# Causal attention then a cosine MLP: every transposition as a pair of 64-row halves, one reciprocal a step, three probability buffers

## The chip, the cores and the metric

The kernel runs on one core of a Trainium2 chip. The metric is the device time of one execution in microseconds (us): median of 3 runs before the change 608.6, lowest 608.53, highest 608.68.

A core has five engines that the text speaks of: PE (TensorE, matrix products and transpositions, which write to the eight banks of the accumulation memory PSUM), DVE (VectorE), ACT (ScalarE), POOL (GpSimd, which here works in SBUF only) and SP, which issues most DMAs. Each takes its instructions in the order written; they meet only through semaphores.

## The reference, cut to what matters

```python
# q, k, v: 4 batches x 12 heads x 448 rows x 64
scores = scale * q @ k.T                      # per batch and head
scores = where(above the diagonal, -1e9, scores)
attn = exp(scores - max(scores)); attn /= attn.sum() + 1e-9
x = (attn @ v)                                # heads side by side: 1792 x 768
h = x @ w_in                                  # 768 x 2048
out = (h * cos(h)) @ w_out                    # 1792 x 768
```

## The kernel before, in words

The work has two stages. The attention stage takes 24 steps, one for each batch and pair of heads; then the MLP stage, a long dense sequence of products on PE, uses the rest of the time. The change touches the attention stage alone. Its order is written out by hand, engine by engine, by the order of the calls in the loop at L477; no scheduler moves anything.

A step treats the 448 rows of two heads in seven row blocks `m` = 1 to 7 of 64 rows each; one head's 64 rows and the other's share the 128 partitions. Block `m` has `64*m` columns, since later keys are masked. The parts of a step `i`, with their names in the code:

- `transpose_in` (L307): PE turns q and k (loaded by `load_qk`, 112 partitions by four rows each) with four transpositions of 112 rows each; `evac_in` (L319) copies each 128x448 result from PSUM to SBUF. In step `i` this is done for step `i+1`.
- `scores` (L345): 16 products q k^T, into banks 4 to 7. Each stands in the trace as two matrix instructions.
- `masked` (L360): DVE adds the mask, writes the block to `prob` and takes the row maxima, one instruction for each block. `exps` (L368): ACT takes the exponential in place and sums the rows.
- `inverse` (L376): DVE adds 1e-9 to the sums and takes the reciprocal, two small instructions; done twice a step, for the blocks `FIRST` = (7, 4, 3) in their own step and for `SECOND` = (6, 1, 5, 2) early in the next. `normalise` (L381): POOL multiplies each block by its reciprocals.
- `tp` (L400): in step `i` PE transposes the 14 squares of 128x128 of step `i-1`'s probabilities, in four groups `ORDER`; `evac_tp` (L408) copies each group out: two of 512 columns on DVE, one of 512 and one of 256 on ACT.
- `av` (L421): in step `i` PE multiplies the transposed probabilities of step `i-2` by v; `finish_hi` (ACT) and `finish_lo` (DVE) split the result.
- At the end of a step the loop yields; the caller (L1357) then puts one half of a weight conversion on DVE (L139 and L142, or L148 and L152), and what is left of it goes to POOL in the next step (`postponed`).

Two `prob` tiles are used in turn. After step 23 the first products of the MLP (`fill`, L464) are put between the remaining parts.

## Time and profile before

| | us |
|---|---|
| median of 3 runs | 608.6 |
| profiled execution, time | 608.03 |
| its span, first to last instruction | 606.2 |
| PE, DVE, ACT, POOL busy in the span | 595.4, 475.7, 409.0, 455.1 |
| granted PE clock, mean | 0.999 of 2.4 GHz |

The attention stage takes about the first 160 us. The profile's views are read thus: a timeline has one row for an instruction, or for a run of equal ones of one engine: start, duration, engine, source line, operation, tiles, shapes, count, and in brackets the idle time before it with what ended it. Instructions of one engine overlap: the next one starts before the last has drained, so what one costs its engine is the distance from its start to the next start. "PEld" are PE's weight loads, which go ahead of the products.

### The profile page before, as it was taken

Reading aid. Unit: us, or ns where it says so; the run is one execution under the profiler, and the core shown is the slowest. Engines: PE = TensorE matmul, PEld = TensorE weight load, DVE = VectorE, ACT = ScalarE, POOL = GpSimd, SP = SyncE. Lnnn points to the kernel's source line nnn. Section 1 sums busy time; section 2 is a strip of 40 time slices with the busy share of each in tenths; the row PEclk is TensorE's granted clock in tenths of the full one; section 3 lists DMA queues with packets and bytes.
Section 4 is the critical chain, followed back from the end, with each engine's and each line's share of the span. In section 5 each row is a group of like instructions: output and inputs, shape, how many; then the busy total and the mean of one; then the engine's idle time right before and its main releaser. Section 6 shows DMA issues by size and latency. Waiting matters only on the chain.

```text
span 606.2 us, 13434 instructions
## 1 busy us (share of the span) xinstructions
PE 595.4 (98%) x4786; PEld 546.6 (90%) x4786; DVE 475.7 (78%) x1020; ACT 409.0 (67%) x925; POOL 455.1 (75%) x527
## 2 busy tenths in 40 slices
PE   7999999999999999999999999999999999999996
PEld 6788888888799998999999999999999999999995
DVE  5999999999477787777777777853387887887786
ACT  4899999999666787777778777632544643654540
POOL 2778887888358788877878777844588778878894
PEclk9999999999999999999999999999999999999999
DMA  6757667758046869796968879589979548658104
GB/s 145 175 132 179 164 141 195 167 137 236 10 138 234 297 228 347 241 340 199 337 241 286 297 225 323 194 323 393 407 297 306 196 148 288 214 168 298 51 0 157
DMA packets 127010, 134.18 MB, mean 221 GB/s; under 512 B 75072, under 2 KB 111280, under 8 KB 126944
## 3 DMA queue, kind: packets, MB, share of 16 engines
q1 hardware_dynamic: 119264, 106.92, 56.4%
q0 software_dynamic: 4928, 24.78, 11.1%
q10 hardware_dynamic: 2752, 1.64, 0.9%
q8 instruction: 38, 0.62, 0.4%
q14 instruction: 28, 0.23, 0.1%
HBM read 83.36 MB, written 49.94 MB: 220 GB/s over the span
## 4 chain that ended last, share of the span: by engine, by line
PE 75%; DVE 21%; issue 2%; DMA 1%; POOL 0%; ACTq 0%; ACT 0%; DVEq 0%; POOLq 0%
PE banks L678 22%; PE banks L1107 13%; PE banks L1127 13%; DVE pb L363 9%; PE banks L583 7%; PE banks L584 7%; PE banks L582 7%; DVE pm L315 4%; PE banks L1144 2%; PE banks L1031 2%; DVE ct L148 1%; DVE xa L460 1%; DVE stat L379 1%; DVE ct L152 1%; DVE ct L139 1%
## 5 line engine op out<-in xcount | busy, mean ns | idle before, releaser
L666 DVE TENSOR_TENSOR acc<-acc,banks 128x768 f32<-128x768 f32 (+1 forms) x122 | 112.7, 932 | 43.3 <-PE banks L678 33.0
L385 POOL TENSOR_TENSOR pb<-pb,stat 128x448 f32<-128x448 f32 (+6 forms) x166 | 101.9, 643 | 34.3 <-DVE stat L379 32.4
L678 PE MATMUL banks<-w,gh 128*128 128x384 f32 x512 | 109.8, 335 | 0.0
L371 ACT ACTIVATE pb<-pb,stat 128x448 f32<-128x448 f32 (+6 forms) x168 | 84.8, 507 | 14.7 <-DVE stat L363 9.4
L678 PEld LDWEIGHTS banks<-w,gh 128*128 128x128 f32 x512 | 90.8, 188 | 1.6 <-DVE acc L666 0.2
L583 PE MATMUL banks<-xa,w 128*128 128x512 f32 x192 | 75.2, 391 | 0.0
L584 PE MATMUL banks<-xa,w 128*128 128x512 f32 x192 | 75.0, 391 | 0.0
L582 PE MATMUL banks<-xa,w 128*128 128x512 f32 x192 | 74.8, 390 | 0.0
L678 PE MATMUL banks<-w,gl 128*128 128x384 f32 x256 | 65.1, 335 | 0.0
L702 POOL TENSOR_TENSOR w<-ct,w 128x768 fp32r<-128x768 f32 x28 | 51.9, 1852 | 14.6 <-ACT w L701 9.4
L363 DVE CUSTOM_DVE_ANT_0 pb<-banks,mask 128x448 f32<-128x448 f32 (+6 forms) x168 | 61.3, 417 | 1.7 <-PE banks L354 1.6
L590 ACT ACTIVATE ni<-banks 128x512 int32<-128x512 f32 (+1 forms) x64 | 34.5, 538 | 32.9 <-PE banks L584 19.1
L609 POOL TENSOR_TENSOR gl<-r,gh 128x512 fp32r<-128x512 f32 x32 | 41.5, 1299 | 19.3 <-ACT gh L608 19.1
L592 DVE SCALAR_TENSOR_TENSOR r<-ni,banks 128x512 f32<-128x512 int32 (+1 forms) x56 | 35.0, 626 | 21.4 <-ACT ni L590 20.7
L403 PE MATMUL banks<-ident,pb 128*128 128x128 f32 x336 | 48.0, 277 | 1.6 <-POOL pb L385 0.9
L594 ACT ACTIVATE r<-r 128x512 f32<-128x512 f32 (+1 forms) x56 | 32.8, 586 | 21.7 <-DVE r L592 21.0
L678 PEld LDWEIGHTS banks<-w,gl 128*128 128x128 f32 x256 | 46.4, 188 | 0.0
L597 DVE SCALAR_TENSOR_TENSOR r<-r,banks 128x512 f32<-128x512 f32 (+1 forms) x56 | 35.1, 626 | 13.9 <-ACT r L595 13.9
L1107 PE MATMUL banks<-xb,bb 128*128 128x384 f32 x234 | 44.7, 334 | 0.0
L354 PE MATMUL banks<-flat 64*64 64x64 f32 (+5 forms) x768 | 42.6, 356 | 1.2 <-DVE stat L379 0.7
L354 PEld LDWEIGHTS banks<-flat 64*64 64x64 f32 x768 | 30.8, 133 | 13.6 <-issue 2.5
L584 PEld LDWEIGHTS banks<-xa,w 128*128 128x128 f32 x192 | 36.0, 188 | 7.5
(139 smaller groups left out, 1492.9 us busy)
## 6 DMA issues: line engine op xcount, KB each, us to landing
bb<-w_in_d SPq DMA_DIRECT2D x48, 384.0 KB, 5.0
land<-in_moe_w_in_dram SPq DMA_DIRECT2D x14, 768.0 KB, 5.5
land<-in_moe_w_out_dram SPq DMA_DIRECT2D x14, 768.0 KB, 5.1
w_out_d<-w POOLq DMA_DIRECT2D x14, 768.0 KB, 5.5
big<-w_out_d SPq DMA_DIRECT2D x25, 384.0 KB, 4.6
w_in_d<-w POOLq DMA_DIRECT2D x7, 768.0 KB, 4.1
raw_d<-ct POOLq DMA_DIRECT2D x14, 384.0 KB, 7.3
land<-in_k_dram SPq DMA_DIRECT2D x46, 112.0 KB, 3.2
```

What stands on the lines that cost most here:

```text
L354: nc.tensor.matmul(place(m)[heads(j ^ SWAP[m]), c : c + z - a], lhsT=qt[heads(j), (m - 1) * R : m * R], rhs=kt[heads(j), a:z], start=banks ...
L363: nc.vector.tensor_tensor_reduce(out=probs(i, m), in0=place(m), in1=mask[:, z : z + m * R], scale=-scale, scalar=3.0e38, op0=ALU.add, op1= ...
L371: nc.scalar.activation(probs(i, m), probs(i, m), AF.Exp, scale=-1.0, bias=st[:, 0, col(m)], accum_out=st[:, 1, col(m)],)
L385: eng.tensor_tensor(p, p, r.to_broadcast(list(p.shape)), op=ALU.mult)
L582: yield nc.tensor.matmul(hv, lhsT=wh[:, f], rhs=x[:, 0, cc, t], start=(cc == 0), stop=False)
L583: yield nc.tensor.matmul(hv, lhsT=wh[:, f], rhs=x[:, 1, cc, t], start=False, stop=False)
L584: yield nc.tensor.matmul(hv, lhsT=wl[:, f], rhs=x[:, 0, cc, t], start=False, stop=(cc == NCC - 1))
L666: nc.vector.tensor_tensor(d, d, o, op=ALU.subtract)
L678: nc.tensor.matmul(o[:, e, 0:EH], lhsT=a[:, cs], rhs=w[:, e * EH : (e + 1) * EH], start=(x == 0), stop=(x == 5),)
L702: nc.gpsimd.tensor_tensor(w[:, 1], tf, f32(w[:, 0]), op=ALU.subtract)
L1107: nc.tensor.matmul(o, lhsT=w[:, u, k * P : (k + 1) * P], rhs=x[k][:, v], start=k + m == 0, stop=k == K - 1 and m == 2,)
L1127: nc.tensor.matmul(o[:, b % 2, 0:EH], lhsT=g_ops[i][u][:, c * P : (c + 1) * P], rhs=wouts[g, i][:, v], start=(x == 0), stop=(x == 2),)
```

## The change

- q and k are loaded on 64 partitions by seven rows each, q on the lower half of the partitions and k on the upper half. `transpose_in` does seven pairs of transpositions of 64 rows; the two of a pair use the two halves of PE's rows and write different banks. It is done two steps ahead (for step `i+2` in step `i`), and the copies out of PSUM, both on ACT, open step `i+1`.
- `tp` is done likewise: each square becomes two transpositions of 64 rows on the two halves, 28 in all, in two groups of seven squares; each group fills two banks, copied out by four copies of 448 columns, two on DVE and two on ACT.
- `inverse` is called once a step, for all seven blocks, when the last `exps` is done; all seven `normalise` follow it. Steps 0 and 1 are written out apart. Three `prob` tiles are used in turn.
- The blocks are taken in the order 4, 3, 7, 6, 5, 1, 2. Up to step 22 the loop yields in the middle of the step, so the weight conversion on DVE stands behind the last `masked`.

```diff
-                nat[i] = [nat_t[0:Q4, 2 * (i % 3) + x] for x in range(2)]
+                nat[i] = nat_t[:, i % 3]
...
-            def transpose_in(i, which, b):
-                for c in range(4):
-                    nc.tensor.transpose(o[:, c], nat[i][which][:, c], ident[0:Q4, 0:Q4])
+            def transpose_in(i, bs, order=None):
+                for c, h in order or [(c, h) for c in range(NM) for h in range(2)]:
+                    o = qkt[i, h][1].rearrange("p (r c) -> p c r", c=NM)
+                    nc.tensor.transpose(o[:, c], nat[i][half(h), c], ident[half(h), half(h)])
...
-            FIRST, SECOND = (7, 4, 3), (6, 1, 5, 2)
+            FIRST, SECOND = (4, 3, 7), (6, 5, 1, 2)
+            ALL = FIRST + SECOND
...
+            GROUPS = [
+                [(6, 0), (7, 0), (6, 1), (7, 1), (6, 2), (7, 2), (3, NM)],
+                [(2, 0), (4, 0), (3, 0), (5, 0), (4, 1), (5, 1), (5, NM)],
+            ]
...
+            def tp(i, g, bs):
+                for x, (m, kc) in enumerate(GROUPS[g]):
+                    for h in range(2):
+                        nc.tensor.transpose(
+                            banks8[:, bs[h], x * R : (x + 1) * R],
+                            prob[i][half(h), a * R : (a + 2) * R], ident[half(h), half(h)],
+                        )
...
+            TB_, G1, G2 = (2, 3), (7, 4), (5, 6)
...
+                elif cur:
+                    if i + 1 < N:
+                        evac_in(i + 1, 0)
+                        evac_in(i + 1, 1)
+                    masked(i, 4, 3, 7, 6, 5, 1, 2)
+                    exps(i, 4, 3, 7, 6, 5)
+                if i < N - 1:
+                    yield i
...
+                if old:
+                    av(i - 2)
+                    finish_hi(i - 2)
+                    finish_lo(i - 2)
+                if cur:
+                    exps(i, 5, 1) if i == 1 else exps(i, 1)
+                if prev:
+                    open_ptr(i - 1)
+                    tp(i - 1, 0, G1)
+                    evac_tp(i - 1, 0, G1, 0, True)
+                    evac_tp(i - 1, 0, G1, 1)
+                if cur:
+                    exps(i, 2)
+                if 1 < i < N - 2:
+                    transpose_in(i + 2, TB_)
+                if prev:
+                    tp(i - 1, 1, G2)
+                    evac_tp(i - 1, 1, G2, 1)
+                if cur:
+                    inverse(i, ALL)
+                    normalise(i, 6, 7, 3, 5, 4, 1, 2)
+                if prev:
+                    evac_tp(i - 1, 1, G2, 0, True)
```

On DVE, before, from the end of one step into the next (`xa`: the attention result, `pm`: transposed probabilities, `ct`: weights, `pb`: `prob`; the row named ISA is `masked`):

```order
L460 TENSOR_TENSOR xa<-banks,xa 128x448
L315 COPY pm<-banks 128x512 x2
L139 TENSOR_SCALAR ct<-st 128x256
L142 SCALAR_TENSOR_TENSOR ct<-st,ct 128x256
L363 ISA pb_145,stat<-banks,mask 128x448
L363 ISA stat 128x1
L378 TENSOR_SCALAR stat<-stat 128x4
L379 RECIPROCAL stat<-stat 128x4
```

The same place after it:

```order
L139 TENSOR_SCALAR ct<-st 128x256
L142 SCALAR_TENSOR_TENSOR ct<-st,ct 128x256
L457 TENSOR_TENSOR xa<-banks,xa 128x448
L317 COPY pm<-banks 128x448
L378 TENSOR_SCALAR stat<-stat 128x7
L379 RECIPROCAL stat<-stat 128x7
L317 COPY pm<-banks 128x448
L363 ISA pb_144,stat<-banks,mask 128x256
```

The conversion has moved ahead of the copies, the two copies are shorter, and the one `inverse` stands between them.

On ACT, one whole step before, from its first exponential to the next step's (`flat`: turned q or k):

```order
L371 ACTIVATE pb_145,stat<-pb_145,stat 128x448
L371 ACTIVATE pb_145,stat<-pb_145,stat 128x256
L371 ACTIVATE pb_145,stat<-pb_145,stat 128x192
L456 CAST xa<-banks 128x448
L317 COPY flat<-banks 128x448
L371 ACTIVATE pb_145,stat<-pb_145,stat 128x384
L317 COPY flat<-banks 128x448
L371 ACTIVATE pb_145,stat<-pb_145,stat 128x64
L371 ACTIVATE pb_145,stat<-pb_145,stat 128x320
L317 COPY pm<-banks 128x512
L371 ACTIVATE pb_145,stat<-pb_145,stat 128x128
L317 COPY pm<-banks 128x256
```

And after:

```order
L371 ACTIVATE pb_146,stat<-pb_146,stat 128x256
L371 ACTIVATE pb_146,stat<-pb_146,stat 128x192
L371 ACTIVATE pb_146,stat<-pb_146,stat 128x448
L371 ACTIVATE pb_146,stat<-pb_146,stat 128x384
L371 ACTIVATE pb_146,stat<-pb_146,stat 128x320
L453 CAST xa<-banks 128x448
L371 ACTIVATE pb_146,stat<-pb_146,stat 128x64
L319 COPY pm<-banks 128x448
L371 ACTIVATE pb_146,stat<-pb_146,stat 128x128
L319 COPY pm<-banks 128x448
L319 COPY flat<-banks 128x448 x2
```

The copies of q and k now stand behind the last exponential, next to the last copy of `pm`.

On PE, a step's transpositions before, between `av` and the next `scores` (`land`: q or k as loaded):

```order
L440 MATMUL banks<-pm,vn_89 64x128 x6
L311 MATMUL banks<-ident,land 128x112 x4
L403 MATMUL banks<-ident,pb_144 128x128 x4
L311 MATMUL banks<-ident,land 128x112 x4
L403 MATMUL banks<-ident,pb_144 128x128 x10
L354 MATMUL banks<-flat 64x64 x2
```

And after:

```order
L437 MATMUL banks<-pm,vn_89 64x128 x6
L402 MATMUL banks<-ident,pb_146 128x64 x14
L313 MATMUL banks<-ident,land 128x64 x14
L402 MATMUL banks<-ident,pb_146 128x64 x14
L354 MATMUL banks<-flat 64x256 x2
```

22 transpositions have become 42 with half the columns.

## Rows read from the trace of the kernel before

**Rows 1.** Busy time of PE, PEld, DVE, ACT, POOL, 40 to 140 us; clock, DMA.

```profile
40.00:140.00 100.00, 99.94 (x1608) 83.52 (x1610) 97.67 (x380) 92.68 (x321) 84.03 (x141) 1.00 0.66 162
```

**Rows 2.** The chain that ended last, share of the span by engine.

```profile
PE 75%; DVE 21%; issue 2%; DMA 1%; POOL 0%; ACTq 0%; ACT 0%; DVEq 0%; POOLq 0%
```

**Rows 3.** Timeline of DVE through one step; start us, us, instruction.

```profile
73.40 0.61 DVE L363 CUSTOM_DVE_ANT_0 pb<-banks,mask 128x448 f32<-128x448 f32 x1
...
73.94 0.16 DVE L378 TENSOR_SCALAR stat<-stat 128x4 f32<-128x4 f32 x1
...
74.25 0.42 DVE L363 CUSTOM_DVE_ANT_0 pb<-banks,mask 128x256 f32<-128x256 f32 x1
...
74.60 0.35 DVE L363 CUSTOM_DVE_ANT_0 pb<-banks,mask 128x192 f32<-128x192 f32 x1
...
76.93 1.28 DVE L315 COPY pm<-banks 128x512 f32<-128x512 f32 x2
78.12 0.76 DVE L148 SCALAR_TENSOR_TENSOR ct<-st,ct 128x256 uint32<-128x256 uint32 x1
...
79.45 0.61 DVE L363 CUSTOM_DVE_ANT_0 pb<-banks,mask 128x448 f32<-128x448 f32 x1
```

**Rows 4.** Timeline of DVE: the first `masked` of steps 2 and 23.

```profile
18.54 0.62 DVE L363 CUSTOM_DVE_ANT_0 pb<-banks,mask 128x448 f32<-128x448 f32 x1
...
146.27 0.61 DVE L363 CUSTOM_DVE_ANT_0 pb<-banks,mask 128x448 f32<-128x448 f32 x1
```

**Rows 5.** DVE's copies out of PSUM: duration ns min/median/max.

```profile
L315 DVE COPY pm<-banks x48: 661/681/692, 17.4 to 157.6; 128x512 f32<-128x512 f32 x48
L315 DVE COPY flat<-banks x4: 608/618/626, 6.5 to 15.9; 128x448 f32<-128x448 f32 x4
```

**Rows 6.** Timeline of ACT through the same step.

```profile
74.05 0.67 ACT L371 ACTIVATE pb<-pb,stat 128x448 f32<-128x448 f32 x1 [0.42 <-DVE stat L363]
...
77.11 0.52 ACT L317 COPY flat<-banks 128x448 f32<-128x448 f32 x1
77.53 0.36 ACT L371 ACTIVATE pb<-pb,stat 128x64 f32<-128x64 f32 x1
...
78.41 0.58 ACT L317 COPY pm<-banks 128x512 f32<-128x512 f32 x1
78.88 0.41 ACT L371 ACTIVATE pb<-pb,stat 128x128 f32<-128x128 f32 x1
79.18 0.20 ACT L371 ACTIVATION_READ_ACCUMULATOR pb<-pb,stat 128x1 f32 x1
```

**Rows 7.** Timeline of PE in the same step: products on halves, transpositions, scores.

```profile
73.56 0.22 PE L429 MATMUL banks<-pm,vn 64*64 64x64 f32 x2
73.56 0.22 PE L429 MATMUL banks<-pm,vo 64*64 64x64 f32 x2
73.62 0.22 PE L429 MATMUL banks<-pm,vn 64*64 64x64 f32 x2
...
75.31 0.60 PE L311 MATMUL banks<-ident,land 112*128 112x112 f32 x4
...
76.70 1.40 PE L403 MATMUL banks<-ident,pb 128*128 128x128 f32 x10
78.03 1.74 PE L354 MATMUL banks<-flat 64*64 64x64 f32 x32
```

**Rows 8.** Timeline of PE's weight loads there: two for transpositions behind a wait.

```profile
77.66 0.20 PEld L403 LDWEIGHTS banks<-ident,pb 128*128 128x128 f32 x2 [0.16 <-DVE pm L315]
```

**Rows 9.** Timeline of POOL in the same step: `normalise`.

```profile
74.45 2.12 POOL L385 TENSOR_TENSOR pb<-pb,stat 128x384 f32<-128x384 f32 x4 [0.62 <-DVE stat L379]
...
77.10 2.15 POOL L385 TENSOR_TENSOR pb<-pb,stat 128x448 f32<-128x448 f32 x3
```

**Rows 10.** Timeline at both ends of the stage: step 1 on DVE; PE's weight loads in step 24.

```profile
13.77 1.08 DVE L385 TENSOR_TENSOR pb<-pb,stat 128x64 f32<-128x64 f32 x2
...
153.72 0.42 PEld L403 LDWEIGHTS banks<-ident,pb 128*128 128x128 f32 x4 [0.35 <-POOL pb L385]
```

More of the change, by code (lines that the diff above doesn't have):

```diff
@@ L236, in attention @@
             NM = S // R
-            Q4 = S // 4
-            nat_t = rows.rearrange("p (t c d) -> p t c d", t=6, d=P)
+            nat_t = rows[:, 0 : 3 * NM * P].rearrange("p (t c d) -> p t c d", t=3, d=P)
             vn_t = [cst.tile([P, NB, P], F32, name=f"vn{i}") for i in range(3)]
@@ L249, in heads, with half @@
                 return slice(j * D, (j + 1) * D)
+            def half(h):
+                return slice(h * R, (h + 1) * R)
             def load_qk(i, *engs):
                 b, hp = pairs[i]
-                nat[i] = [nat_t[0:Q4, 2 * (i % 3) + x] for x in range(2)]
-                for dst, src in zip(nat[i][::-1], (k, q)):
+                nat[i] = nat_t[:, i % 3]
+                for h, src in ((1, k), (0, q)):
                     for j, eng in enumerate(engs or (nc.sync, nc.sync)):
                         eng.dma_start(
-                            out=dst[:, :, heads(j)],
-                            in_=src[b, 2 * hp + j].rearrange("(p c) d -> p c d", c=4),
+                            out=nat[i][half(h), :, heads(j)],
+                            in_=src[b, 2 * hp + j].rearrange("(p c) d -> p c d", c=NM),
                         )
@@ L291, in attention @@
             make_identity(nc, ident)
-            prob_t = [cst.tile([P, NM * (NM + 1) // 2 * R], F32, name=f"pb{i}") for i in range(2)]
+            prob_t = [cst.tile([P, NM * (NM + 1) // 2 * R], F32, name=f"pb{i}") for i in range(3)]
             mask = cst.tile([P, S + W], F32, name="mask")
@@ L317, in evac, with evac_in @@
                     nc.scalar.copy(dst, src)
-            def evac_in(i, which, dve=False, rs=slice(0, Q4)):
-                d, s = qkt[i, which]
-                d = d.rearrange("p (r c) -> p r c", c=4)
-                s = s.rearrange("p (r c) -> p r c" if which else "p (c r) -> p r c", c=4)
-                evac(d[:, rs], s[:, rs], dve)
+            def evac_in(i, h, dve=False):
+                evac(*qkt[i, h], dve)
             AT = {5: 0, 1: 5, 3: 6, 7: 9, 6: 16, 4: 22, 2: 26}
@@ L334, in open_step @@
             def open_step(i):
-                prob[i] = prob_t[i % 2]
+                prob[i] = prob_t[i % 3]
                 stats[i] = at.tile([P, 3, 8], F32, tag="stat", bufs=3, name="stat")
@@ L469, in fill, with tail @@
                     pass
-            transpose_in(0, 1, 7)
+            def tail(i, *ms):
+                inverse(i, ms)
+                normalise(i, *ms)
+            TB_, G1, G2 = (2, 3), (7, 4), (5, 6)
+            transpose_in(0, TB_, [(c, 1) for c in range(NM)])
             evac_in(0, 1)
             keep_warm(14)
-            transpose_in(0, 0, QB)
+            transpose_in(0, TB_, [(c, 0) for c in range(NM)])
             evac_in(0, 0, True)
             keep_warm(8)
+            load_qk(2)
             for i in range(N + 4):
-                cur, prev, nxt = i < N, 0 < i <= N, i + 1 < N
-                old = 0 <= i - 2 < N
-                if i + 2 < N:
-                    load_qk(i + 2)
+                cur, prev, old = i < N, 0 < i <= N, 0 <= i - 2 < N
+                if i >= N - 1:
+                    G1, G2 = (2, 3), (4, 5)
+                if i + 3 < N:
+                    load_qk(i + 3)
                 if prev:
@@ L486, in attention @@
                     scores(i)
[L487 to L488 removed]
                 if i == 0:
                     masked(i, 4, 3)
[L491 to L496 removed]
+                    exps(i, 4, 3)
+                    masked(i, 7, 6)
+                    exps(i, 7)
@@ L574, in attention @@
-                yield i
+                    normalise(i, 7, 3, 4)
+                    exps(i, 5, 1, 2)
+                    transpose_in(2, (0, 1))
+                    yield i
+                    continue
+                if i == 1:
+                    masked(i, 4, 3, 7, 6)
+                    inverse(i - 1, SECOND)
+                    normalise(i - 1, *SECOND)
+                    masked(i, 5, 1, 2)
+                    evac_in(2, 0, True)
+                    evac_in(2, 1, True)
+                    exps(i, 4, 3, 7, 6)
+                elif cur:
[4 more added lines that the diff above has]
+                    exps(i, 4, 3, 7, 6, 5)
@@ L576, in m1_sum @@
+                if i >= N - 1:
+                    yield i
     def m1_sum(ring, g, fi, t0, n, hv):
```

136 lines of the change are left out of this document (28 added, 108 removed).

## The prediction

> **What bounds the kernel now.** I read four views in this order. First the busy times of a steady stretch of the attention stage, 40 to 140 us [rows 1]: PE is shown busy for 99.94 of 100 us, VectorE (DVE) for 97.67, ScalarE (ACT) for 92.68, POOL for 84.03. PE's figure overlaps pipelined products, so it does not settle who binds. Then the chain that ended last [rows 2]: DVE holds 21% of the span, 127 us, though in the dense MLP stage PE carries the chain; so in the attention stage it runs through DVE. Then DVE's timeline [rows 3]: from one first `masked` at 73.40 to the next at 79.45 are 6.05 us with instruction after instruction and no idle time noted. Last, the start of the first `masked` of step 2 and of step 23 [rows 4]: 127.73 us for 21 steps, 6.08 each. The steady stage is bound by DVE's own work, with ACT about 0.45 us a step behind it and PE able to follow.
>
> **The change, part by part.**
>
> *DVE loses 0.43 us a step.* An `inverse` (two instructions) costs from 73.94 to 74.25, 0.30 us beside what any hand-over takes [rows 3]; one of two goes. Its three or four columns become seven, which I cost at nothing: it is the fixed part of a small instruction. The two copies of `pm` take 1.19 us of DVE (76.93 to 78.12), 0.60 each; a copy of 448 columns is 0.06 shorter than one of 512 (618 against 681 ns) [rows 5], so two save 0.13. DVE alone would then need 6.05 - 0.43 = 5.62 us a step. The moved weight conversion costs DVE the same wherever it stands.
>
> *ACT gains 0.1 us a step.* Its copies out of PSUM were two of 448, one of 512 and one of 256; they become four of 448. A 448 takes 0.42 (77.11 to 77.53), a 512 0.47 (78.41 to 78.88) [rows 6]; the 256 is an estimate of 0.3, between half and the whole of a 448; so the sum goes from 1.6 to 1.7 us.
>
> *A ring between DVE and ACT closes.* The single `inverse` waits for the last exponential of its own step, and behind it on DVE wait the last copy of `pm`, the next step's `masked` and so ACT's next exponentials. The ring: `masked` of block 4, 74.25 to 74.60, 0.35; its read-out and the hand-over to ACT, 0.11 (the 448 block leaves DVE at 73.94 and ACT starts at 74.05) [rows 3, 6]; ACT from its first exponential to the end of its last; hand-over to DVE, taken as half of the 0.11; `inverse` 0.30; a 448 copy, 0.60 - 0.06 = 0.53. ACT's part is read from its stretch 74.05 to 79.38 (79.18 + 0.20), 5.33 us, which holds seven exponentials, the cast of the result, two 448 copies and a 512 [rows 6]. In the new order only one 448 copy stands inside, so 5.33 - 0.42 - 0.47 = 4.44. Sum: 0.35 + 0.11 + 4.44 + 0.05 + 0.30 + 0.53 = 5.78 us. That is above DVE's own 5.62, so it sets the step: 0.30 less than 6.08, and over the 21 steps 6.3 us. DVE then waits some 0.16 us a step at `inverse`.
>
> *PE's transpositions: off the path, but their price must be bounded.* Before, 22 of them, each 0.11 us from start to start (four in 0.60 with 0.27 for one), take with their waits from 75.31 to 78.03, 2.72 us of the step; all else of PE takes 6.05 - 2.72 = 3.33 [rows 7]. The nearest rows for pairs on two halves are the 64-row products of L429: the upper-half product (`vo`) starts at the same 73.56 as the lower (`vn`), and the next lower one 0.06 later. So 21 pairs would cost 21 x 0.06 = 1.3 us, and PE would need 4.6 to 5.0 us a step. The other end: halves that take turns, 42 x 0.06 = 2.5 us. I take the first, as the row shows both halves at work at once; being of 64 columns, it does not show it for loads of 128. Since PE isn't in the ring, its 1 us saved counts for nothing.
>
> The Trainium skill says so of such a change in general (TensorEngine Tiling (Array Packing), PSUM Bottleneck): tiling makes TensorE faster, not the copies out of PSUM. Here the trace agrees as far as it goes, DVE at 97.67 of 100; a sum that credited PE's saving would be 21 us lower.
>
> *POOL* has the same seven `normalise`, now in one batch of 2.12 + 2.15 = 4.3 us [rows 9], and the same rest of the weights. Its load is 0.84 x 6.08 = 5.1 us a step [rows 1], under 5.78, and the three `prob` tiles let `tp` of a step wait for it until the middle of the next. I cost it at nothing; if that cover went, POOL's lateness would hold up PE's second group and then ACT's last copy.
>
> *SP and the loads.* Same number of loads, one step more of them at the start, with landings a step ahead of use: nothing.
>
> *The ends of the stage.* Step 1 loses two `normalise` on DVE, 1.08 us [rows 10]; I take 1.1 off. At the end the seven `normalise` of step 23 stand before `tp` of that step, where PE already waited 0.35 us for four of them [rows 10]: POOL has 2 us more to do before the last square, but PE has products of the MLP to put there and DVE reaches that `inverse` earlier. Between a loss of 2 and a gain of 1, nearest to the row: 0.
>
> *Sum* against the profiled execution's own time, 608.0: 608.0 - 6.3 - 1.1 = 600.6. The median of the runs is 0.6 above that execution, so 601.2 us.
>
> **The rivals.**
>
> *A wait through PE closes a longer ring (slower).* DVE's last copy of `pm` frees bank 5; if all the next scores came behind it, the ring would be: copy 0.62, scores and `av` 3.33, then on ACT the cast 0.42, an exponential 0.36, a copy 0.42 and the last exponential 0.50, `inverse` 0.30, and three hand-overs of 0.1: 6.25 us a step, 0.17 x 21 = 3.6 us more, and without the gain in step 1 612.2 us. It decides from the point at which more than half of the scores wait for that copy: by the new order the first five of eight blocks' products go to banks that are freed earlier, and what stands behind is block 6, 2 and 1, some 0.75 of the 1.5 us of scores, which makes the ring 5.5. For it: bank 5 is the last freed, and block 6, which goes there, is the fourth that `masked` asks for. Against: 0.28 us of room. If it binds in part, a step is near 5.95: 605.
>
> *The halves take turns (slower).* PE would need 3.33 + 42 s + 0.39 of waits as now (2.72 - 22 x 0.106): with s = 0.06, 6.24 us a step, so + 3.4 - 1.1: 610.9 us. It decides from s = 0.056 upwards. Against: the pair at 73.56. For: no row has loads of 128 columns on two halves.
>
> The Trainium skill has a rule that would make it far worse (TensorE: Matmul & The Clock Gate, LDWEIGHTS): a weight load takes its columns at 1.2 GHz, whatever its rows, so 0.107 us for 128 columns; 42 in turn would be 4.5 us and the kernel near 650, and if the halves' loads overlap, 2.25 us and the forecast stands. The trace speaks against the figure: two such loads stand within 0.20 us at 0.14 each, so the second began 0.06 after the first [rows 8].
>
> *PE was the bound after all.* Then a step loses the whole 1.0 to 1.4 us: 21 us or more, 586. For it, 99.94 of 100; against it, DVE's row without a gap. *The change of PE's load lowers its clock*: the granted clock is 1.00, of 2.4 GHz, in the stretch [rows 1], and the pauses to come are under 1 us; I give it nothing of its own.
>
> *DVE alone binds*, ACT slipping out of the ring by running ahead: 5.62 us, 597.8; it lies in the forecast's own range.
>
> **How the numbers follow.** Chances: the DVE-ACT ring or a little beside it, 0.78 (own range 597.8 to 604.4: steps of 5.62 to 5.90, where the last has the first 0.7 us of the start lost); the ring through PE, 0.12, of which three quarters in part (605) and the rest in full (612); halves in turn 0.08; PE bound 0.02. The range, 597.8 to 605.8, leaves out the slower cases and PE's. A difference under 0.2%, 1.2 us, can't be told from none: same is 607.4 to 609.8. Faster: 0.77 + 0.07 + 0.02 = 0.86; same 0.06, from parts of both slower cases; slower 0.08.
>
> **What would show it.** Right: steps of 5.7 to 5.9 us from first `masked` to first `masked`; a wait of DVE for ACT before L378 or of ACT for DVE before the first exponential, and little else; lower and upper halves of L402 starting within 0.01 us of each other, pairs 0.06 apart; PE with idle time in each step; the MLP stage's length unchanged. Wrong: `masked` or the cast of the result waiting for PE (the longer ring), transpositions 0.06 apart singly (turns), DVE still without a gap at 6.0 us or more (its instructions grew), or `tp` waiting for POOL in each step.

## The result, and the profile after

| | us |
|---|---|
| predicted | 601.2 (597.8 to 605.8) |
| measured, median of 4 runs | 614.14 (611.85 to 614.63) |
| against before (608.62) | ratio 1.0080, 95% interval 1.0064 to 1.0096 |
| profiled execution, time and span | 614.63 and 612.6 |

The kernel became 0.8% slower. The spans differ by 6.4 us, in three places. The first `masked` of steps 2 and 23 stand in DVE's timeline after the change thus (start, duration, instruction):

```profile
20.11 0.42 DVE L363 CUSTOM_DVE_ANT_0 pb<-banks,mask 128x256 f32<-128x256 f32 x1 [1.12 <-PE banks L354]
...
150.35 0.42 DVE L363 CUSTOM_DVE_ANT_0 pb<-banks,mask 128x256 f32<-128x256 f32 x1 [0.43 <-PE banks L354]
```

Against [rows 4]: the start took 1.57 us more (20.11 against 18.54), the 21 steps 2.51 more (130.24 against 127.73, 6.20 a step instead of 6.08), and from there to the end of the span 2.34 more (462.2 against 459.9).

**The steady steps.** Busy time of the same 100 us as [rows 1], same columns:

```profile
40.00:140.00 100.00, 84.81 (x1924) 72.40 (x1916) 88.75 (x347) 92.63 (x316) 84.84 (x139) 1.00 0.70 165
```

DVE fell from 97.67 to 88.75 and PE from 99.94 to 84.81; ACT stands where it was. No engine is full, and yet a step is longer: it goes round in a ring, a chain of waits over several engines that comes back one step later to the instruction it began with. One step on DVE after the change, where [rows 3] showed no gap:

```profile
73.62 0.62 DVE L457 TENSOR_TENSOR xa<-banks,xa 128x448 fp32r<-128x448 f32 x1 [0.33 <-ACT xa L453]
74.17 0.61 DVE L317 COPY pm<-banks 128x448 f32<-128x448 f32 x1
74.78 0.17 DVE L378 TENSOR_SCALAR stat<-stat 128x7 f32<-128x7 f32 x1
74.98 0.20 DVE L379 RECIPROCAL stat<-stat 128x7 f32<-128x7 f32 x1
75.10 0.57 DVE L317 COPY pm<-banks 128x448 f32<-128x448 f32 x1
76.02 0.42 DVE L363 CUSTOM_DVE_ANT_0 pb<-banks,mask 128x256 f32<-128x256 f32 x1 [0.34 <-PE banks L354]
...
79.78 0.62 DVE L457 TENSOR_TENSOR xa<-banks,xa 128x448 fp32r<-128x448 f32 x1 [0.18 <-ACT xa L453]
```

DVE waits twice: 0.33 for ACT's cast ahead of the subtraction L457, and 0.34 for PE ahead of the first `masked`. PE and ACT in the same step, answering to [rows 6, 7] (PE's first and last row are cut off by the window, at 12 and 8 of 14):

```profile
72.80 0.53 PE L313 MATMUL banks<-ident,land 64*128 64x64 f32 x12
73.61 0.65 PE L402 MATMUL banks<-ident,pb 64*128 64x64 f32 x14 [0.28 <-POOL pb L385]
74.83 1.81 PE L354 MATMUL banks<-flat 64*64 64x256 f32 x29 [0.57 <-DVE pm L317]
...
78.35 0.65 PE L402 MATMUL banks<-ident,pb 64*128 64x64 f32 x14
78.83 0.60 PE L313 MATMUL banks<-ident,land 64*128 64x64 f32 x14
79.92 0.46 PE L402 MATMUL banks<-ident,pb 64*128 64x64 f32 x8 [0.48 <-POOL pb L385]
```

```profile
76.48 0.51 ACT L371 ACTIVATE pb<-pb,stat 128x256 f32<-128x256 f32 x1 [0.46 <-DVE stat L363]
...
79.23 0.52 ACT L453 CAST xa<-banks 128x448 fp32r<-128x448 f32 x1
```

PE is idle 0.57 us until DVE's copy of `pm` frees bank 7. The ring can be read off these rows: subtraction 0.55 (73.62 to 74.17), first copy 0.61, hand-over 0.05, from the first product of the scores to the first `masked` 1.19 (74.83 to 76.02), to ACT 0.46, five exponentials 2.75 (76.48 to 79.23), cast and hand-over 0.55, and the next subtraction starts at 79.78: 6.16 us. Counted from `masked` to `masked`, steps of 6.04 and 6.21 take turns in the first half of the stage; most of the difference is that in every other step `masked` follows the first product after 1.07 instead of 1.19. The same rows confirm what was said of PE: 14 transpositions on two halves take 0.65 and 0.60 us, where ten of the old ones took 1.40.

**The start.** PE in step 1, and the granted clock of three stretches (the last three columns are the clock as a share of 2.4 GHz, the DMA share, GB/s):

```profile
13.59 0.65 PE L313 MATMUL banks<-ident,land 64*128 64x64 f32 x14
16.03 0.86 PE L402 MATMUL banks<-ident,pb 64*128 64x64 f32 x14 [1.80 <-POOL pb L385]
17.32 1.01 PE L402 MATMUL banks<-ident,pb 64*128 64x64 f32 x14 [0.42 <-POOL pb L385]
```

```profile
9.50:16.28 6.78, 4.74 (x104) 3.87 (x95) 6.32 (x35) 6.54 (x25) 3.10 (x5) 1.00 0.74 146
16.28:23.10 6.82, 6.40 (x90) 5.16 (x88) 4.93 (x21) 5.36 (x19) 5.03 (x10) 0.50 0.64 153
23.10:30.00 6.90, 6.53 (x158) 5.70 (x156) 5.47 (x22) 5.85 (x20) 4.31 (x7) 1.00 0.69 159
```

PE stood idle 1.80 us for POOL, and right behind that pause the clock fell to half (1.2 GHz) for 6.8 us. Before, PE stood 0.94 at this place, and the clock is 1.00 in all three stretches; the row and the middle one of the three:

```profile
14.76 0.88 PE L403 MATMUL banks<-ident,pb 128*128 128x128 f32 x6 [0.94 <-POOL pb L385]
```

```profile
16.28:23.10 6.82, 6.75 (x101) 5.31 (x100) 6.70 (x29) 5.92 (x21) 4.71 (x8) 1.00 0.79 187
```

The 1.57 us are not all of one kind. The first `masked` of step 0 already starts at 9.27 instead of 8.33; in the other kernels built on the changed one it does so anywhere between 8.57 and 9.58, by their profiled executions, and the pause comes only later. From the first `masked` of step 1 to that of step 3, a stretch that holds the pause and the half clock, it is 14.02 us after the change, against 12.78 before. Three of the four executions of the new kernel have a mean clock of 0.992 to 0.994 over the span, the fastest, 611.85, has 0.996; before has 0.999.

**The rest** is in the MLP stage, most of it late: counted from step 23, ACT's instructions run about 0.9 us behind those of the kernel before from 260 to 437 us, and 2.6 behind from 450 on. Between 437 and 456 us POOL waits 2.1 us for `raw` to land, DVE 1.3 for `xb`; the second wait stands in e3_warm too, whose stage is 2 us shorter.

```profile
POOL tr L1043 <- DMA raw<-raw_d: 2.1, 1, 2.1
...
DVE acc L646 <- DMA xb<-t_d: 1.3, 1, 1.3
```

### The profile page after: what moved, and what is told of

Its sections match the earlier page's. It is cut to its first block, busy times and chain, and to the rows that moved or that the text cites. A ratio compares the mean times of both kernels' runs of the same rounds, so it can differ in the third digit from the quotient of the medians.

```text
span 612.6 us, 14289 instructions
## 1 busy us (share of the span) xinstructions
PE 580.3 (95%) x5266; PEld 534.8 (87%) x5266; DVE 464.2 (76%) x972; ACT 411.4 (67%) x925; POOL 459.0 (75%) x529
## 3 DMA queue, kind: packets, MB, share of 16 engines
q10 hardware_dynamic: 2752, 1.64, 1.0%
## 4 chain that ended last, share of the span: by engine, by line
PE 70%; ACT 14%; DVE 10%; DMA 2%; POOL 2%; issue 2%; SPq 0%; DVEq 0%; ACTq 0%; POOLq 0%
PE banks L660 17%; PE banks L1109 12%; PE banks L1089 12%; ACT pb L371 10%; PE banks L565 6%; PE banks L566 6%; PE banks L564 6%; PE banks L354 4%; PE banks L1126 2%; PE banks L1013 2%; DVE pm L317 2%; DVE pb L363 2%; DVE xa L457 2%; DMA big<-w_out_d 1%; ACT xa L453 1%
## 5 line engine op out<-in xcount | busy, mean ns | idle before, releaser
L385 POOL TENSOR_TENSOR pb<-pb,stat 128x448 f32<-128x448 f32 (+6 forms) x168 | 104.7, 658 | 34.8 <-DVE stat L379 33.0
L371 ACT ACTIVATE pb<-pb,stat 128x256 f32<-128x256 f32 (+6 forms) x168 | 84.2, 504 | 14.7 <-DVE stat L363 14.7
L363 DVE CUSTOM_DVE_ANT_0 pb<-banks,mask 128x256 f32<-128x256 f32 (+6 forms) x168 | 60.0, 420 | 9.5 <-PE banks L354 9.5
L354 PE MATMUL banks<-flat 64*64 64x64 f32 (+5 forms) x768 | 45.6, 368 | 11.7 <-DVE pm L317 11.2
L354 PEld LDWEIGHTS banks<-flat 64*64 64x64 f32 x768 | 35.7, 136 | 21.6 <-DVE pm L317 13.3
L1109 PE MATMUL banks<-big,gh 128*128 128x384 f32 x168 | 42.6, 334 | 0.0
```

What stands on the lines that cost most here:

```text
L354: nc.tensor.matmul(place(m)[heads(j ^ SWAP[m]), c : c + z - a], lhsT=qt[heads(j), (m - 1) * R : m * R], rhs=kt[heads(j), a:z], start=banks ...
L363: nc.vector.tensor_tensor_reduce(out=probs(i, m), in0=place(m), in1=mask[:, z : z + m * R], scale=-scale, scalar=3.0e38, op0=ALU.add, op1= ...
L371: nc.scalar.activation(probs(i, m), probs(i, m), AF.Exp, scale=-1.0, bias=st[:, 0, col(m)], accum_out=st[:, 1, col(m)],)
L385: eng.tensor_tensor(p, p, r.to_broadcast(list(p.shape)), op=ALU.mult)
L1109: nc.tensor.matmul(o[:, b % 2, 0:EH], lhsT=g_ops[i][u][:, c * P : (c + 1) * P], rhs=wouts[g, i][:, v], start=(x == 0), stop=(x == 2),)
```

## The experiments

Medians; the ratio is to the kernel before in the same batch. Step 2: start of its first `masked`; step: mean of the 21 behind it, both from the profiled execution.

| run | us | ratio, 95% | step 2 | step |
|---|---|---|---|---|
| before | 608.6 | | 18.54 | 6.08 |
| after | 614.14 | 1.0080 (1.0064 to 1.0096) | 20.11 | 6.20 |
| e1_4_3_first | 610.91 | 1.0029 (1.0009 to 1.0050) | 19.83 | 6.15 |
| e2_copy_first | 606.41 | 0.9955 (0.9939 to 0.9972) | 19.85 | 5.89 |
| e12_both | 604.44 | 0.9927 (0.9910 to 0.9945) | 18.92 | 5.90 |
| e3_warm | 610.06 | 1.0020 (1.0010 to 1.0029) | 18.75 | 6.16 |
| e4_copy_first_warm | 604.79 | 0.9925 (0.9909 to 0.9942) | 19.28 | 5.90 |
| e5_turns | 611.40 | 1.0037 (1.0024 to 1.0050) | 19.00 | 6.16 |
| e6_two_inverses | 612.60 | 1.0061 (1.0046 to 1.0076) | 19.25 | 6.26 |
| e7_bank7_by_act | 603.88 | 0.9917 (0.9902 to 0.9931) | 18.28 | 5.89 |
| e8_bank7_no_add | 601.68 | 0.9879 (0.9862 to 0.9897) | 18.23 | 5.87 |
| e9_warm_no_add | 609.38 | 1.0016 (1.0005 to 1.0027) | 18.83 | 6.16 |
| e10_before_no_add | 603.37 | 0.9917 (0.9899 to 0.9935) | 18.07 | 5.87 |
| e11_4_with_2 | 612.60 | 1.0070 (1.0054 to 1.0086) | 20.85 | 6.19 |
| e13_4_2_first | 609.77 | 1.0019 (1.0010 to 1.0029) | 21.73 | 6.03 |
| e14_v_first | 601.51 | 0.9879 (0.9863 to 0.9896) | 18.48 | 5.74 |
| e15_inverse_sooner | 612.10 | 1.0052 (1.0037 to 1.0067) | 18.17 | 6.16 |
| e16_all | 602.97 | 0.9893 (0.9872 to 0.9915) | 18.19 | 5.74 |

### Is it the ring through the first copy?

e2_copy_first moves one call on the changed kernel; e12_both adds the edit of e1.

```diff
                     finish_hi(i - 2)
-                    finish_lo(i - 2)
...
                     evac_tp(i - 1, 0, G1, 0, True)
+                if old:
+                    finish_lo(i - 2)
...
```

> On DVE the first copy of pm goes ahead of the subtraction of the result (L457), nothing else is moved. Theory (ring through the first copy): the subtraction's 0.55 us, its wait of 0.33 for ACT's cast and the cast leave the ring, so the scores of the next step may start up to 0.8 us sooner; a step falls to about 5.8 us, where ACT's own 5.75 holds it: about 606. Rival P (POOL and PE's second group): no change, 614. Rival L (last copy): no change, the last copy keeps its place.

> Both edits: products of blocks 4 and 3 first, and the first copy of pm ahead of the subtraction. Theory: the ring through PE is then far below ACT's own 5.75 us and below the DVE-ACT ring of 5.78 that was forecast, so little beyond either edit alone: steps of about 5.75 to 5.8, 605. Rival P: 614. If a ring of another kind remains in each single edit, this one falls below both.

Steps of 5.89 and 5.90 instead of 6.20, for one DVE instruction put behind its neighbour. In the 6.20 stands one step of 6.89 at half clock; with the clock kept in both (e4_copy_first_warm against e3_warm) it is 5.90 against 6.16, 0.26 less. The rivals of POOL and of the last copy predicted no change. DVE's wait has changed its place; in e12_both it stands where the prediction had put it:

```profile
78.06 0.41 DVE L363 CUSTOM_DVE_ANT_0 pb<-banks,mask 128x256 f32<-128x256 f32 x1
...
81.51 0.61 DVE L317 COPY pm<-banks 128x448 f32<-128x448 f32 x1
82.04 0.61 DVE L457 TENSOR_TENSOR xa<-banks,xa 128x448 fp32r<-128x448 f32 x1
83.02 0.17 DVE L378 TENSOR_SCALAR stat<-stat 128x7 f32<-128x7 f32 x1 [0.36 <-ACT pb L371]
83.22 0.20 DVE L379 RECIPROCAL stat<-stat 128x7 f32<-128x7 f32 x1
83.34 0.57 DVE L317 COPY pm<-banks 128x448 f32<-128x448 f32 x1
83.86 0.42 DVE L363 CUSTOM_DVE_ANT_0 pb<-banks,mask 128x256 f32<-128x256 f32 x1
```

```profile
78.57 0.51 ACT L371 ACTIVATE pb<-pb,stat 128x256 f32<-128x256 f32 x1 [0.16 <-DVE stat L363]
...
82.79 0.19 ACT L371 ACTIVATION_READ_ACCUMULATOR pb<-pb,stat 128x1 f32 x1
```

From `masked` at 78.06 to `masked` at 83.86 it is 5.80 us, through ACT (78.57 to 82.98) and the one `inverse`, for which DVE waits 0.36. Both edits together gave no shorter step than the second alone, as expected if another ring then binds; but the 5.75 to 5.8 expected for it are met only by every other step (5.80 and 5.96 in turn).

e7_bank7_by_act leaves the subtraction where it was and frees bank 7 otherwise (on e3_warm, with e1's order of products):

```diff
-            TB_, G1, G2 = (2, 3), (7, 4), (5, 6)
+            TB_, G1, G2 = (2, 3), (4, 7), (5, 6)
```

> On e3_warm with the products in the order of e1_4_3_first: the two banks of the first group of transpositions are exchanged, so that ACT's copy (some 0.3 us sooner in the trace of the changed kernel) frees bank 7 and DVE's first copy, still behind the subtraction, frees bank 4. Theory (the ring closes because blocks 4 and 3, the first that masked asks for, wait in bank 7 for DVE's first copy, and masked waits for both): steps fall to about 5.9 us with the subtraction where it was, 604.5 us. Rival (e2_copy_first gained because DVE no longer stood 0.33 us before the subtraction waiting for ACT's cast): no change against e3_warm, 610.

5.89 us, 603.88. Two different cuts of the same ring give the same step, and e1's order of products, which e7 has besides, is worth 0.06 by itself (below); that the ring ran through bank 7 and DVE's first copy is shown.

### What lies in the 1.19 us from products to `masked`?

```diff
-                    (4, 0, 0, 4 * R), (7, 0, 6 * R, 7 * R), (7, R, 0, 6 * R), (3, 0, 0, 3 * R),
+                    (4, 0, 0, 4 * R), (3, 0, 0, 3 * R), (7, 0, 6 * R, 7 * R), (7, R, 0, 6 * R),
```

> The products of the scores go in the order 4, 3, 7, 7, 5, 6, 2, 1 instead of 4, 7, 7, 3, ... Theory (the ring of 6.16 us a step goes through the subtraction L457, the FIRST copy of pm, the scores of the blocks in bank 7, the first masked and ACT's exponentials): the first masked no longer waits for the 448 columns of block 7; it starts about 0.77 us after the first product instead of 1.19, so a step falls from 6.20 to about 5.8 us (ACT's own work, 0.926 x 6.20 = 5.75 us, is the next floor), 21 x 0.4 = 8 us: about 606. Rival P (PE's second group of transpositions, which waits for POOL's normalise in every step, sets the step): no change, 614. Rival L (DVE's last copy of pm, bank 5): no change, since block 6 stays where it is in the row of products.

A miss: 0.06 us a step, not 0.4. The first `masked` starts 1.13 us after the first product (87.42 against 86.29). The products that PE started in the first 0.2 us tell why (L354, durations in ns, span of the starts, shapes with counts):

```profile
L354 PE MATMUL banks<-flat x8: 218/347/485, 86.3 to 86.5; 64*64 64x64 f32 x4, 64*64 64x256 f32 x2, 64*64 64x384 f32 x2
```

Both parts of block 7 (64 and 384 columns) have begun, and nothing of block 3 (192 columns), which stands ahead of them in the program. Blocks 4 and 3 use the same two quarters of the array and follow one another; block 7 uses the other two and runs beside them. Read from the single records, block 3's last product ends 0.97 us after the first one of the step, here as in the changed kernel: its place in the program had not delayed it. The next two runs exchange blocks 2 and 3 in PSUM, so that 4 has the shorter neighbour; e13 issues that neighbour ahead of 7. Both have the thirty products of e3_warm (see The start).

```diff
-            BANK = {..., 2: (6, 5), 4: (7, 0), 3: (7, 4)}
+            BANK = {..., 2: (7, 4), 4: (7, 0), 3: (6, 5)}
...
-                    (4, ...), (7, ...), (7, ...), (3, ...), (5, ...), (6, ...), (2, ...), (1, ...),
+e11:                (4, ...), (7, ...), (7, ...), (2, ...), (5, ...), (6, ...), (3, ...), (1, ...),
+e13:                (4, ...), (2, ...), (7, ...), (7, ...), (5, ...), (6, ...), (3, ...), (1, ...),
...
-                    masked(i, 4, 3, 7, 6, 5, 1, 2)
-                    exps(i, 4, 3, 7, 6, 5)
+                    masked(i, 4, 7, 6, 5, 3, 1, 2)
+                    exps(i, 4, 7, 6, 5, 3)
```

> On e3_warm: blocks 2 and 3 exchange their places in PSUM, so block 4 shares its bank with block 2 (128 columns) and no longer with 3 (192); masked and the exponentials take 3 behind 5. Theory (masked of block 4 waits until the last product of its bank; blocks whose products use the same two quarters of the array run one behind the other, so what stands behind 4 in its bank counts, not where block 7 stands): the first masked starts about 0.11 us sooner after the first product (1.08 instead of 1.19), the steps fall from 6.16 to about 6.05, 607.7. Rival (the 1.19 us are a fixed time from the first product to a masked): no change, 610.

> As e11_4_with_2 (blocks 2 and 3 exchanged in PSUM, 612.6 us, steps of 6.09 and 6.21), with the products in the order 4, 2, 7, 7, 5, 6, 3, 1. Theory (PE reports its products in the order of issue, so masked of block 4 waits for the end of all that is issued up to the last product of its bank; blocks on the same quarters of the array run one behind the other, those on the other quarters beside them): the two products of 2 end 0.87 us after the first product, where 7 or 3 ended at 0.98 to 0.99 in e1_4_3_first and e11_4_with_2; the first masked starts 1.02 to 1.06 after the first product instead of 1.18, steps fall by 0.12 to 0.15, 609.4 to 610. Rival (a fixed time, not these products): 612.6.

e11 missed: by the single records block 2 ended 0.87 us after the first product, but `masked` still came at 1.18 (88.62 against 87.44), 0.19 after the end of block 7, which is issued ahead of 2. With 2 issued ahead of 7, e13:

```profile
86.72 1.76 PE L354 MATMUL banks<-flat 64*64 64x256 f32 x26 [0.37 <-DVE pm L317]
```

```profile
87.74 0.42 DVE L363 CUSTOM_DVE_ANT_0 pb<-banks,mask 128x256 f32<-128x256 f32 x1 [0.18 <-PE banks L354]
```

1.02 us, and steps of 6.03 instead of 6.19. The semaphore that `masked` of block 4 waits for is raised by the last product of bank 7. In e11 the trace has it raised 1.05 us after the first product, not at 0.87 where that product ends; in e13 at 0.89. So `masked` waits for the end of all products issued up to the last one of its bank: 0.99 us in the changed kernel and in e11, 0.87 in e13, and a hand-over of 0.15 to 0.20 behind it (0.05 to 0.08 in the steps between). (Steps 0 and 1 of both kernels still ask for block 3 second, hence, it seems, their late step 2; in e13 the half clock adds to it.)

### The start

e3_warm fills the pause; e4_copy_first_warm is e2 with it; e15_inverse_sooner shortens it.

```diff
                 if i == 1:
                     transpose_in(i + 2, TB_)
+                    keep_warm(30, 7)     # 30 products of 128x128 into bank 7
```

```diff
-                    masked(i, 4, 3, 7, 6)
+                    masked(i, 4, 3)
                     inverse(i - 1, SECOND)
                     normalise(i - 1, *SECOND)
+                    masked(i, 7, 6)
```

> Thirty small products (128x128 bf16) stand on PE in step 1 ahead of the first transpositions of the probabilities, where PE was idle for 1.80 us before the granted clock fell to half from 16.3 to 23.1 us; the steady steps are untouched. Theory (that pause starts the stretch at half clock, which costs about 2 of the 5.5 us lost): no half-clock stretch, first masked of step 2 at about 18.5 instead of 20.1, 612. Rival (the clock falls for the light work of the steps behind it, not for the pause): the stretch stays, 614 or a little more.

> The changed kernel (614.1) with one edit: in step 1 the second inverse of step 0 and its normalise stand behind two masked instead of four, as near as in the kernel before; no warming products. Theory (the pause of 1.80 us on PE in step 1 comes from POOL starting late, and the half clock follows that pause): POOL's block 6 starts at about 14.1 instead of 15.15, the pause shrinks to about 0.75, no half clock behind it, first masked of step 2 at 18.5 to 19 instead of 20.1, 610 to 611. Rival (the half clock comes from the light work in the steps behind): it stays, 613.

e3_warm has no half clock at the start and step 2 at 18.75; its ten runs lie within 0.84 us. e15 without added products, PE in step 1:

```profile
13.35 0.74 PE L313 MATMUL banks<-ident,land 64*128 64x64 f32 x14 [0.40 <-DMA land<-in_q_dram]
14.86 0.65 PE L402 MATMUL banks<-ident,pb 64*128 64x64 f32 x14 [0.77 <-POOL pb L385]
16.14 0.65 PE L402 MATMUL banks<-ident,pb 64*128 64x64 f32 x14 [0.64 <-POOL pb L385]
```

A pause of 0.77, no half clock, step 2 at 18.17. From the first `masked` of step 1 to that of step 3 it is 12.14 us in e3_warm and 12.04 in e15, against 14.02: the edits take back 1.9 and 2.0 us, so the pause with the half clock behind it carried that loss, and the later `inverse` of step 0 made the pause. The rest of e15's early step 2 is its early step 0 (8.57 against 9.27). e3_warm's 610.06 lies 2 us under the 612 expected, and its MLP stage is 2 us shorter (460.2 against 462.2), which its edit does not touch. e15's time is 1 to 2 us above what was expected, because its MLP stage came out as long as the changed kernel's (462.6 us from step 23 on, against 460.2 in e3_warm): what sets that length is open; the attention's steps are the same in both.

> The first copy of pm ahead of the subtraction (as in e2_copy_first) and the thirty small products in step 1 (as in e3_warm). Theory: the two losses have different places (the ring of the steady steps; the pause in step 1 that ends in half clock), so the gains add up: e2_copy_first 606.4 less the 4.1 that e3_warm took off, 602.3 us, steps of 5.88, no half-clock stretch at the start. Rival (the half clock also explained part of what e2_copy_first gained): 604 to 606.

604.79, not 602.3, and in the rival's range. The clock was kept, but of the 4.1 us that e3_warm took off, 2 were those of the MLP stage, which in e2_copy_first was already at 461.5 and here takes 461.1. And e2 had less to win back: its clock was at half for 3.4 us instead of 6.8, and from step 1 to step 3 it took 12.70 instead of 14.02, here 11.72. Step 2 came 0.5 later than in e3_warm because step 0 did (9.58 against 9.06).

### PE's pairs, and the one reciprocal

e5_turns takes the pairs apart; e6_two_inverses undoes the single reciprocal on e4_copy_first_warm.

```diff
-                for x, (m, kc) in enumerate(GROUPS[g]):
+                for h in range(2):        # all seven of one half, then of the other
...
-                    for h in range(2):
+                    for x, (m, kc) in enumerate(GROUPS[g]):
```

```diff
                     evac_tp(i - 1, 0, G1, 0, True)
+                if cur:
+                    inverse(i, (4, 3, 7, 6, 5))
+                    normalise(i, 6, 7, 3, 5, 4)
...
-                    inverse(i, ALL)
-                    normalise(i, 6, 7, 3, 5, 4, 1, 2)
+                    inverse(i, (1, 2))
+                    normalise(i, 1, 2)
```

> On e3_warm (610.06): the transpositions of a group are issued seven of one half and then seven of the other, instead of by turns, so no two neighbours lie on different halves. Theory (pairs on two halves run at once only as neighbours, and PE's saving lies beside the ring): the 14 of L402 and of L313 go from 0.65 and 0.60 us to about 0.9 to 1.0 each, PE's idle time shrinks by as much, the time stays within 1 us of 610.06. Rival (PE's transpositions are on the path): three groups a step by 0.3 us, 20 us more.

The group of 14 takes 0.89 us instead of 0.65 (not twice as long: by the single records the two sevens overlap from the fifth product on), the steps stay at 6.16; the 1 us that it lost on e3_warm (by the two ratios) lies outside them. PE's saving was worth nothing to the steps.

> On e4_copy_first_warm: two inverses a step again, the first over blocks 4, 3, 7, 6, 5 behind the first copy of pm, with their normalise on POOL right behind it; the second over 1 and 2 where the single one was. Theory (after e2_copy_first the steps go by the ring of DVE and ACT, in which one inverse stands; the other takes DVE's free 0.2 to 0.35 us a step): POOL starts about 1 us sooner, PE's waits for POOL go, the time is the same or up to 2 us longer than e4_copy_first_warm. Rival P (the wait of PE's second group for POOL sets the step): faster by 0.25 to 0.38 us a step, 5 to 8 us.

A miss in size: 7.8 us slower. PE's waits for POOL did go (its loads waited 2.7 us in 40 to 140 us instead of 8.4) and brought nothing, against rival P. But each of the small additions L378 takes 426 or 494 ns on average, where the single one takes 262 in e4_copy_first_warm and 171 in the changed kernel. Rows of DVE, then POOL, at one of them:

```profile
92.75 0.58 DVE L457 TENSOR_TENSOR xa<-banks,xa 128x448 fp32r<-128x448 f32 x1
93.25 0.60 DVE L378 TENSOR_SCALAR stat<-stat 128x2 f32<-128x2 f32 x1
93.89 0.17 DVE L379 RECIPROCAL stat<-stat 128x2 f32<-128x2 f32 x1
```

```profile
93.00 0.83 POOL L385 TENSOR_TENSOR pb<-pb,stat 128x384 f32<-128x384 f32 x1 [0.42 <-DVE stat L379]
```

The addition of two columns starts behind a `normalise` that began at 93.00 and ends with it, at 93.85 against 93.83. That these waits make the whole 0.36 us a step was not tested; the two additions take 0.92 us a step where the one took 0.26.

### What binds once that ring is cut

L378 adds 1e-9 to sums that hold at least the 1 of their maximum; without it the float32 result is the same.

```diff
-                nc.vector.tensor_scalar(st[:, 2, cs], st[:, 1, cs], 1e-9, None, op0=ALU.add)
-                nc.vector.reciprocal(st[:, 2, cs], st[:, 2, cs])
+                nc.vector.reciprocal(st[:, 2, cs], st[:, 1, cs])
```

> The same deletion of L378 on e3_warm (610.06), whose scores are as in the changed kernel. Theory (there the ring passes through the subtraction, the FIRST copy and PE; L378 stands behind that copy and ends before the scores, beside the ring): 0.2 us of DVE's work a step less and no gain, 609.5 to 610.1; DVE's wait for PE before the first masked grows by 0.2. Rival (DVE's own work, or the ring with inverse in it, sets these steps): 21 x 0.2 = 4.2 us less, 606.

> On e7_bank7_by_act (603.88): the small addition of 1e-9 in front of each reciprocal (L378) is left out; each sum of exponentials holds the 1 of its own maximum, so in float32 the addition changes no bit. Theory (with the ring through PE gone, the ring of DVE and ACT that was forecast at 5.78 sets the step, at 5.80 and 5.96 in turn; the 5.96 is the step in which L378 takes 0.41 instead of 0.17, because it stands behind POOL's L157): both kinds of step get shorter and stop at ACT's own 5.76 us; 21 x 0.12 = 2.5 us, 601.4. Rival (POOL's normalise and PE's second group set what is left): no change, 603.9.

> The deletion of L378 on the kernel before (two of them a step, 0.16 and 0.18 us, 0.4 with their hand-overs). Theory (the kernel before is bound by DVE's own work, as the prediction read it): a step falls from 6.07 by 0.3 to 0.4, about 6 to 8 us in all: 601 to 603. Rival (before stood in a ring through PE as well, and DVE's row without gaps hid it): less than 2 us, 607 to 608.7.

The same deletion gives nothing to e3_warm's steps (6.16), where it stands beside the ring; 2.3 us to e7, by the two ratios; and 5.3 to the kernel before, whose steps fall from 6.08 to 5.87. The last is a little short of the 6 to 8 forecast, with ACT then at 98.7 of 100 us; it speaks for the prediction's reading that before was bound by DVE's own work. By the ratios the kernel before without the addition (0.9917) is as fast as the changed kernel with its ring cut (e7, 0.9917). In e8 three steps were held up by a load:

```profile
PE banks L425 <- DMA vn<-in_v_dram: 2.5, 4, 1.2
```

```diff
-                if i + 3 < N:
-                    load_qk(i + 3)
                 if prev:
                     load_v(i - 1)
+                if i + 3 < N:
+                    load_qk(i + 3)
```

> On e8_bank7_no_add (601.68; most steps 5.72 to 5.75, but three of 5.89, 6.88 and 7.42 us, in which PE waited for vn to land): in each step the loads of v are issued ahead of those of q and k, which wait on SP's queue for PE. Theory (the late v stood behind the waiting q and k): no wait for vn, all steps about 5.74, 21 x 0.12 = 2.6 us less, 599. Rival (the DMA engines, busy 0.73 of the time, can't bring it sooner): waits for vn or for land stay, 601 to 602.

> e14_v_first with the edit of e15_inverse_sooner in place of the thirty warming products. Theory: the gains add up; about 1 us at the start below e14_v_first, 598. Rival (without the warming products the clock falls at the start): 600 or more.

```profile
40.00:140.00 100.00, 94.36 (x2047) 77.59 (x2046) 94.80 (x354) 99.05 (x335) 90.65 (x148) 1.00 0.75 185
```

Steps of 5.74 us with ACT busy 99.05 of 100: ACT's own floor. The profile answers the expectation, the time does not: 601.51 is hardly less than e8's 601.68, whose profiled execution, 603.75, was the longest of its four (600.38 at the least). e16 has the same steps and a profiled execution of 600.5, but its other three runs are near 603 at a lower mean clock (0.996 to 0.997); whether the missing warming products are the cause is open. The best version is e14_v_first, 1.2% under the kernel before and by the two ratios 2.0% under the changed one; 0.8% can be had by the deletion of L378 alone (e10).

## Why the prediction was wrong

- **The failed step is the ring between DVE and ACT.** It went from the last copy of `pm` straight to the next `masked`, as if the scores were always ready. "The first five of eight blocks' products go to banks that are freed earlier" holds against bank 5, and I looked at no other; block 4, the first that is asked for, stands in bank 7, which DVE's first copy frees, and that copy stood behind the subtraction, which waits for ACT's cast behind five exponentials. Left out were the subtraction, the first copy and 1.19 us of scores. The ring is 6.16 us, not 5.78, and 6.16 is also the mean step where the clock is kept (e3_warm): 21 x 0.38 = 8.0 us of the miss.
- The forecast ring exists: 5.80 us in every other step of e12_both, with ACT's part 4.41 (78.57 to 82.98) against 4.44 reckoned, and `inverse` 0.32 against 0.30. In the other steps, 5.96, L378 takes 0.41 instead of 0.17: it starts at 77.01 and ends at 77.42, with POOL's L157 (76.66 to 77.39):

```profile
77.01 0.41 DVE L378 TENSOR_SCALAR stat<-stat 128x7 f32<-128x7 f32 x1 [0.21 <-ACT pb L371]
```

```profile
76.66 0.73 POOL L157 TENSOR_TENSOR w<-ct,w 128x256 fp32r<-128x256 f32 x1
```

- The rival "a wait through PE closes a longer ring" was the right kind at the wrong place; it was given 0.12. That its price, 6.25 a step, lies near the 6.20 measured is luck: it goes through bank 5 and has other terms. Of the signs named, `masked` waiting for PE (0.34) is what the trace shows. `tp` waiting for POOL in each step (0.28, 0.48) shows as well, but was not on the path: in e4_copy_first_warm PE's loads still wait 8.4 us for POOL in 40 to 140 us (8.7 in the changed kernel) and the steps are 5.90, and in e6, where these waits shrink to 2.7, nothing is gained.
- DVE's own work fell to 88.75 x 0.0620 = 5.50 us a step, more than forecast (5.62), and counted for nothing while that ring stood. PE's pairs are 0.06 apart as taken from [rows 7], also for loads of 128 columns, and the two of a pair start within 0.004 us of each other; so "halves take turns" fell, and e5 shows that PE's saving too counted for nothing.
- **The start**: -1.1 reckoned, +1.57 measured. 2.7 us of the miss, and 0.9 more in the 21 steps (6.20 against 6.16), most of it in the first, at half clock (6.89 against 6.14 in e3_warm). The two `normalise` taken from DVE went to POOL, behind an `inverse` that stands behind four `masked` instead of three (1.65 us after the first instead of 1.17); PE waited 1.80 us for them, and the half clock to which the prediction gave "nothing of its own" followed. The pauses are "under 1 us" in the steady steps (0.57 in the rows above), not in step 1. By e3_warm, pause and half clock make 1.9 of these 3.6 us (1.1 in step 1, 0.8 in the next). Another 0.9 is the later start of step 0 in that execution, and 0.7 is a saving reckoned and not found: with the clock kept (e3_warm) step 1 is 0.36 us shorter than before, where 1.1 was taken off.
- **The end of the span**: 0 reckoned, +2.3 measured (with 8.0, 2.7 and 0.9 these make 13.9 of the 14.0 between 600.6 and the profiled 614.63), in the MLP stage, 1.7 of it about where POOL waits 2.1 for `raw`. Kernels with the same attention steps (e3_warm, e9_warm_no_add) don't have it (460.2, 459.6); what sets it is open.

The Trainium skill's rule of 0.107 us for a load of 128 columns (TensorE: Matmul & The Clock Gate, LDWEIGHTS), weighed in the prediction, is not what these rows show: 14 such loads, seven on each half, take 0.51 us, where seven in a row would take 0.75 by it.

```profile
73.61 0.51 PEld L402 LDWEIGHTS banks<-ident,pb 64*128 64x128 f32 x14 [0.41 <-POOL pb L385]
```

## What to carry to other kernels

Where one engine's idle time is taken away, write the next ring out to the end: for the first instruction of the step, ask which bank it reads, what filled that bank, what had to empty it, and what that stood behind on its engine. A saving in an engine's busy time is worth nothing until it is in that ring; here one call moved behind its neighbour was worth 21 x 0.26 us, and the savings of DVE and PE nothing as long as the ring stood. And an instruction that does nothing (here the addition of 1e-9) is cheap only off the ring: its deletion gave e3_warm's steps nothing and the kernel before 5.3 us, about as much as the whole change with its ring cut (e7).

## What the runs showed of the hardware

- **Side by side, but reported in order.** Products of 64 rows and 64 columns on different quarters of the array run at once; PE starts them ahead of earlier ones that wait for their own quarters (block 7 at 0.03 us ahead of 3 at 0.48 in e1), but the signal of a product comes only when all issued before it have ended (e11: raised at 1.05 us, e13: 0.89). So for PE "in the order written" holds of the signals and not of the starts.
- **A pause and the clock.** In step 1 the clock fell to half behind pauses of PE of 1.80 us (after), 1.64 (e1), 1.61 (e2) and 1.33 (e12), and behind one of 1.90 in e13, though products followed it, for 3.4 to 6.8 us; behind 0.77 (e15) and 1.04 (e16), and where products filled the pause (e3), it stayed at 1.00 in the profiled executions. But e11 has a pause of 1.92 with the same products behind it as e13, and there too the clock stayed at 1.00: the length of the pause alone does not settle it.
- **DVE and POOL.** The addition L378 on 2 to 7 columns takes 0.17 us, or up to 0.69 behind a running POOL instruction, whose end it then shares (rows of e6 and e12). Not every small DVE instruction waits: in e6 the reciprocal at 93.89 takes 0.17 beside the next `normalise`. The weight conversion's L139, 0.67 us before, is 0.30 in e6, where POOL's `normalise` is nearly over by then. The Trainium skill says (SBUF — State Buffer, Who interferes with whom) that DVE in its two-port modes and POOL take turns at a shared pair of ports for whole instructions; the rows agree in that the addition ends with the POOL instruction it met, but none shows in which mode an instruction ran. What the prediction called DVE's work held such waits (L139).
